# End of an attention and spectral-filter kernel: other order of the output projections' products, other banks for the last memory terms, last rows stored by halves of columns

## Chip, cores and metric

One core of one Trainium2 chip runs the kernel. The metric is device time in microseconds, the median of three executions. One further execution was recorded by the hardware profiler; its page and trace are what is quoted here.

## What is computed

Two independent parts on one input sequence of 2048 rows and 576 columns each, concatenated. Part A is attention with 32 heads of width 18 in four segments of 512 rows, with a running memory M, z, and an output projection with `wo`:

```python
for s in range(N):                      # 4 segments
    qs, ks, vs = q[:, :, s], k[:, :, s], v[:, :, s]
    logits = jnp.einsum("bhqd,bhkd->bhqk", qs, ks) * scale + mask
    p = _softmax(logits, axis=-1)
    a_dot = jnp.einsum("bhqk,bhkd->bhqd", p, vs)
    pq = phi(qs)
    num = jnp.einsum("bhld,bhde->bhle", pq, M)
    den = jnp.einsum("bhld,bhd->bhl", pq, z)[..., None] + 1e-6
    a_mem = num / den
    o = g * a_mem + (1.0 - g) * a_dot
    ...                                 # M, z take in this segment's keys and values
return o @ wo
```

Part B is `irfft2(rfft2(x) * W)`, a filter in the two-dimensional spectrum. The change touches part A alone.

## The kernel before

**Stages.** Forward transform of part B; the projections q, k, v of part A beside the middle of part B; the inverse transform; and then the attention, from `attention` (line 925), which runs to the end of the program. The instructions of each engine stand in the order in which the Python code issues them (a manual schedule); the framework adds the semaphore waits and assigns buffers. Nothing is moved at run time: an engine whose next instruction waits holds up everything behind it on that engine.

**The attention loop.** 133 steps t (lines 947 to 1014), one per head up to step 127. A step interleaves, on TensorE: `s1` (row maxima for the head ten steps ahead), `s2` (line 679: scores with the maximum subtracted, three banks p0, p1, p2 from the tag "s2", which ScalarE turns into exponentials P at lines 688, 693, 697), `pv` (line 708: P times values) and a background list that `run_bg` steps through. The background list holds, for each finished segment, `combine` (line 803: o = memory term plus scaled attention, in five tiles of up to 126 rows, the last of 72), `mem1` (line 786: the next segment's memory terms: the product pn, copied by ScalarE, then pb, the reciprocal spread over the head's rows, multiplied by VectorE) and `oproj` (line 847: the output projection).

**Two words for each value.** The projections keep about 24 bits: o and `wo` are each split in a high word and the rest, so a block is three products, oh x woh, oh x wol and ol x woh, for each of the five tiles t. oh is ScalarE's cast of the combined tile (line 817; line 872 in the last segment), ol the difference that VectorE (or GpSimd) makes behind it (lines 812 and 876). `oproj` has four row blocks `tb` by two column halves `hf` of 288 columns: 15 products into one bank, with a point after the eighth at which other work is put in.

**The last segment.** It has no attention left to hide behind. `last_tile` (line 864) makes o for one tile: pb, two VectorE steps, the cast to oh, and, one tile later, ol through `last_low`. `last_proj` (line 884) issues the three products of accumulator u and tile t. Eight accumulators u (four row blocks by two halves) are open at once: 0 to 2 in the banks of tag "s1", 3 in "pv", 4 to 6 in "s2", 7 in "post". The order is tile 0 for u = 0 to 6, then tile 1, then tile 2 (with the `last_tile` of tiles 3 and 4 put in), then tile 3, then u = 7 for tiles 0 to 3, then tile 4 for all eight; behind each accumulator's last product ScalarE (even u) or VectorE (odd u) copies it to a row block in SBUF, and after each odd one SP stores the row block of 128 x 576.

**Banks.** TensorE's results lie in eight banks: three of tag "s1", three of "s2", one "pv", one "post". `bank` (line 783) gives `oproj`, `combine` and `mem1` a bank of "post" while the step number `s.now` is under 119, and one of "s1" after that. A new use of a bank waits for the engine that reads the old one.

**Queues.** SP issues all loads and stores of this part in program order; a DMA whose source is not ready holds up those behind it on SP.

Of the kernel before, what the change touches and what calls it, by code (L numbers as in the profile page):

```python
# [5 lines left out]
F32=mybir.dt.float32; F32R=mybir.dt.float32r  # L6
# [96 lines left out]
class FFT:  # L103
# [4 lines left out]
    def forward(s,xp,cp,pp,wl,xs,consts):  # L108
# [26 lines left out]
        def f1(u):  # L135
            p=pp.tile([128,2,512],F32,name="f1",tag="f1")
            h,l=eh.pop(u),el.pop(u)
            for r in range(2):
                L=[(h[:,r,0],tab[:,0,r,0]),(h[:,r,1],tab[:,0,r,1]),(h[:,r,0],tab[:,1,r,0]),(h[:,r,1],tab[:,1,r,1]),
                   (l[:,r,0],tab[:,0,r,0]),(l[:,r,1],tab[:,0,r,1]),(h[:99,r,2],tab2[:99,r])]  # L140
                for n,(x,t) in enumerate(L):
                    nc.tensor.matmul(p[:,r,:FP],x,t,start=n==0,stop=n==6)  # L142
# [59 lines left out]
    def bf(s,x,y,inv):  # L202
# [4 lines left out]
        for o,a,b,op in ((t[0],x[0],x[2],OP.add),(t[1],x[0],x[2],OP.subtract),(t[2],x[1],x[3],OP.add),(t[3],x[1],x[3],OP.subtract),  # L207
# [3 lines left out]
            yield  # L211
    def tws(s,L,inv):

        nc=s.nc; v=nc.vector; A=[]; L=[x for x in L if x[1]]
        if not L: return
        for i in range(len(L)+1):
            if i<len(L):
                y,e=L[i]; a=-2*np.pi*e/16*(-1 if inv else 1)
                if i%2==0: T=s.tp.tile([128,2,2,FP],F32,name="tw",tag="t",bufs=4)
                t=T[:,i%2]  # L220
                nc.scalar.activation(t[:,0],y[:,1],AF.Copy,scale=-float(np.sin(a)))
                nc.scalar.activation(t[:,1],y[:,0],AF.Copy,scale=float(np.sin(a)))
                A.append((y,t,float(np.cos(a))))
                if i==0: yield
            if i>0:
                y,t,c=A.pop(0)
                v.scalar_tensor_tensor(y,y,c,t,op0=OP.mult,op1=OP.add)
                yield
# [161 lines left out]
class ATT:  # L390
# [391 lines left out]
        lane.append(chain())  # L782
    def bank(s,name,r=126):

        return (s.ps if s.now<119 else s.ps1).tile([r,512],F32,name=name,tag="post" if s.now<119 else "s1")
    def mem1(s,g,t):
        nc=s.nc; r=126 if t<4 else 72
        pn=s.bank("pn")
        nc.tensor.matmul(pn[:r],s.Mst[g][:r,t,:r],s.pq.pop((g,t))[:r],start=True,stop=True)
        am=s.tp.tile([126,512],F32,name="am",bufs=5)  # L790
        nc.scalar.copy(am[:r],pn[:r])
        if g<3: s.later(1,lambda: s.pq_load(g+1,t))
        yield
        pb=s.bank("pb")
        nc.tensor.matmul(pb[:r],s.sel[:,t,:r],s.rc["rd"],start=True,stop=True)
        nc.vector.tensor_tensor(am[:r],am[:r],pb[:r],op=OP.mult)
        s.am[t]=am; s.amg[t]=g
        yield
# [48 lines left out]
    def oproj(s,g):  # L847
        nc=s.nc
        oh,ol=s.oh,s.ol
        for tb in range(4):  # L850
            ob=s.tp.tile([128,576],F32,name="ob")
            c=slice(128*tb,128*tb+128)
            for hf in range(2):
                ps=s.bank("po",128)[:,:288]
                w=slice(288*hf,288*hf+288)
                L=[(a,b,t) for a,b in ((oh,s.woh),(oh,s.wol),(ol,s.woh)) for t in range(5)]
                for i,(a,b,t) in enumerate(L):
                    r=126 if t<4 else 72
                    nc.tensor.matmul(ps,a[t][:r,c],b[:r,t,w],start=i==0,stop=i==14)  # L859
                    if i==7: yield  # L860
                nc.scalar.copy(ob[:,w],ps)
                if hf==1: s.later(1,lambda tb=tb,ob=ob: nc.sync.dma_start(s.io["ya"][g*512+128*tb:g*512+128*tb+128],ob))
                yield
# [14 lines left out]
    def last_parts(s):  # L878
# [2 lines left out]
        c=c.rearrange("p a b -> p (a b)")  # L881
        s.oh=[a[:,t] for t in range(4)]+[c[:,:512]]; s.ol=[b[:,t] for t in range(4)]+[c[:,512:]]
        s.lows=[]; s.acc={}
    def last_proj(s,u,t):

        nc=s.nc; tb,hf=divmod(u,2); c=slice(128*tb,128*tb+128); w=slice(288*hf,288*hf+288); r=126 if t<4 else 72
        if t==0: s.acc[u]=(s.ps1 if u<3 else s.ps).tile([128,512],F32,name="po",tag="s1" if u<3 else "pv" if u==3 else "s2" if u<7 else "post")[:,:288]
        for i,(a,b) in enumerate(((s.oh,s.woh),(s.oh,s.wol),(s.ol,s.woh))):
            nc.tensor.matmul(s.acc[u],a[t][:r,c],b[:r,t,w],start=t==0 and i==0,stop=t==4 and i==2)  # L889
    def later(s,k,f):  # L890

        s.late.append((s.now+k,f))
# [32 lines left out]
    def attention(s,tp,ps):  # L925
        nc=s.nc; s.tp,s.ps,s.psm,s.mtag=tp,ps,s.ps1,"s1"
# [19 lines left out]
        for t in range(133):  # L946
# [24 lines left out]
            a=s.s1(t+10) if t+10<128 else iter(())  # L971
            b=s.s2(t) if t<128 else iter(())
# [5 lines left out]
            r=(t-5)%4  # L978
# [4 lines left out]
            if t==129:  # L983
                for j in range(4): s.pv(31,j)
                s.pv_out(31)
                u=s.u_dmas(15)
# [6 lines left out]
            if 7<=t<131 and t%4==3:  # L993
                s.pv_out((t-7)//4)
                if t%8==3:
                    u=s.u_dmas((t-11)//8)
# [31 lines left out]
                s.last_proj(u,t)  # L1028
                if t==2 and u in (1,4): s.last_tile(3 if u==1 else 4,"re")
        s.last_low()  # L1030
        for u in range(7): s.last_proj(u,3)
        for t in range(4): s.last_proj(7,t)
        o=[s.tp.tile([128,4,512],F32,name=f"P{i}").rearrange("p a b -> p (a b)") for i in range(2)]
        o=[o[tb//3][:,576*(tb%3):576*(tb%3)+576] for tb in range(4)]
        nc=s.nc
        for u in range(8):
            tb,hf=divmod(u,2); s.last_proj(u,4)
            (nc.vector.tensor_copy if hf else nc.scalar.copy)(o[tb][:,288*hf:288*hf+288],s.acc[u])
            if hf: nc.sync.dma_start(s.io["ya"][1536+128*tb:1664+128*tb],o[tb])

def prio(tc,gen,off):

# [99 lines left out]
```

## Time and profile before

| | us |
|---|---|
| median of 3 executions | 714.35 |
| lowest, highest | 713.14, 716.41 |
| profiled execution, as timed | 714.98 |
| its span, first to last instruction | 713.3 |
| last product on TensorE starts | 709.25 |
| last copy out of a bank starts, takes | 709.65, 0.46 |

In a timeline row stand the start, the duration (a matmul's includes its way through the array, so rows of matmuls overlap), engine, line, operation, result and operands, shapes, how many, and in square brackets how long the engine stood idle before it and which instruction released it. In the chain of waits stand start, length and what ran. A row of the windows gives a stretch, its length, the busy time of TensorE, its weight loads (PEld), VectorE (DVE), ScalarE (ACT) and GpSimd (POOL), the granted TensorE clock, the share of the 16 DMA engines that was busy, and GB/s. The granted clock was 1.00 from 640 to 691 us and 0.99 from 691 to 713.

### The profile page before, as it was taken

The page shows a single profiled execution, that of the slowest core. Times are in us where ns is not written, and L with a number is a line of the kernel's source. Part 1 is how long each engine was busy: PE and PEld are TensorE (multiplying, and loading weights), DVE is VectorE, ACT ScalarE, POOL GpSimd, SP SyncE. Part 2 cuts the span into 40 slices and gives each one's busy share as a digit, 9 for nine tenths or more (in the row PEclk, how much of TensorE's full clock was granted, in tenths as well). Part 3 has the DMA queues.
Part 4 walks back from the last instruction along what each step waited for, and adds up shares of the span by engine and source line. Part 5 has one row for each costly group of instructions (what it writes and reads, how often), then busy time and mean ns, then how long its engine had stood idle before and what let it go on. Part 6 is the DMA issues. An engine that isn't in the chain of part 4 may idle for free.

```text
span 713.3 us, 14181 instructions
## 1 busy us (share of the span) xinstructions
PE 678.1 (95%) x4867; PEld 498.7 (70%) x4867; DVE 553.9 (78%) x1227; ACT 444.5 (62%) x1000; POOL 209.8 (29%) x409
## 2 busy tenths in 40 slices
PE   4999999999999999999999999999999999998997
PEld 3999779879889889999744444444566445664677
DVE  5999989989899887887588878887666876668153
ACT  3657796585584564444387777777656776568631
POOL 2110000100100211565065434545242762237200
PEclk9999999999999999999999999999999999999999
DMA  9877436555463568889637666677547765341331
GB/s 322 276 233 216 142 125 201 189 171 172 158 221 127 164 220 270 214 235 210 172 105 181 169 162 154 175 177 175 133 121 181 170 167 131 103 138 43 99 100 66
DMA packets 83244, 121.04 MB, mean 170 GB/s; under 512 B 11352, under 2 KB 50630, under 8 KB 83036
## 3 DMA queue, kind: packets, MB, share of 16 engines
q1 hardware_dynamic: 76580, 104.11, 51.8%
q0 software_dynamic: 6592, 16.03, 7.9%
q8 instruction: 38, 0.62, 0.4%
q14 instruction: 34, 0.28, 0.1%
HBM read 81.78 MB, written 38.24 MB: 168 GB/s over the span
## 4 chain that ended last, share of the span: by engine, by line
PE 67%; DVE 12%; DMA 7%; ACT 7%; issue 5%; POOL 2%; SPq 0%; DVEq 0%; ACTq 0%; POOLq 0%
PE pv L717 10%; PE pj L464 9%; PE pjv L464 8%; PE po L859 7%; PE s L644 5%; PE s L652 4%; PE i L300 3%; DMA yb<-yout 3%; PE s L687 3%; PE i L311 3%; DVE junk L648 3%; PE s L691 2%; PE po L889 2%; DMA xin<-xb 2%; PE c L163 2%
## 5 line engine op out<-in xcount | busy, mean ns | idle before, releaser
L648 DVE CUSTOM_DVE_ANT_0 junk<-s,mask 128x512 bf16<-128x512 f32 (+1 forms) x256 | 141.8, 554 | 56.4 <-PE s L644 45.4
L654 DVE TENSOR_REDUCE mx<-s 128x4 f32<-128x512 f32 x128 | 87.9, 687 | 17.2 <-PE s L653 15.5
L688 ACT ACTIVATE P<-s 128x512 f32<-128x512 f32 x128 | 77.2, 603 | 23.3 <-PE s L687 20.6
L717 PE MATMUL pv<-P,vs 128*32 128x512 f32 (+3 forms) x1024 | 82.0, 438 | 0.0
L693 ACT ACTIVATE P<-s 128x512 f32<-128x512 f32 x128 | 77.0, 601 | 6.8 <-PE s L692 3.6
L697 ACT ACTIVATE P<-s 128x256 f32<-128x256 f32 x128 | 49.6, 388 | 50.1 <-PE s L696 50.0
L700 POOL TENSOR_SCALAR_AFFINE_SELECT P<-P 128x512 f32<-128x512 f32 x116 | 69.5, 636 | 6.2 <-ACT P L688 6.0
L717 PEld LDWEIGHTS pv<-P,vs 128*32 128x32 f32 x1024 | 26.8, 109 | 44.6 <-issue 41.9
L464 PE MATMUL pj<-x,wqkh 128*128 128x512 f32 x162 | 56.0, 406 | 0.0
L514 POOL MEMSET vt<- 128x32 f32 x16 | 2.4, 162 | 149.6 <-PE pm L524 122.3
L210 DVE TENSOR_TENSOR t<-Z 128x580 f32<-128x580 f32 x64 | 46.2, 757 | 0.1
L210 DVE TENSOR_TENSOR Z<-t 128x580 f32<-128x580 f32 x64 | 45.9, 755 | 0.0
L644 PE MATMUL s<-Ks,Qs 108*128 108x512 bf16 (+1 forms) x128 | 42.2, 329 | 0.0
L142 PE MATMUL f<-ftab,eh 128*128 128x290 f32 (+1 forms) x160 | 31.3, 314 | 10.4 <-DMA ftab<-ftab 10.4
L300 PE MATMUL i<-civ,Y 128*128 128x256 f32 (+1 forms) x288 | 37.8, 284 | 0.8 <-DVE T L332 0.8
L488 ACT CAST sp<-pj 128x512 bf16<-128x512 f32 x36 | 21.1, 586 | 27.0 <-DVE pj L484 27.0
L311 PE MATMUL i<-itab,T 128*128 128x290 f32 (+1 forms) x224 | 36.6, 312 | 1.0 <-DVE yout L319 1.0
L669 POOL CAST mh<-mg 128x16 bf16<-128x16 f32 x32 | 6.9, 216 | 101.1 <-ACT mg L667 69.2
L300 PEld LDWEIGHTS i<-civ,Y 128*128 128x128 f32 (+1 forms) x288 | 35.8, 181 | 1.0 <-DVE T L332 1.0
L464 PE MATMUL pj<-xh,wqkh 128*128 128x512 f32 x90 | 35.6, 395 | 0.0
L464 PEld LDWEIGHTS pj<-x,wqkh 128*128 128x128 f32 x162 | 30.4, 188 | 7.4 <-issue 0.6
L464 PE MATMUL pj<-x,wqkl 128*128 128x512 f32 x90 | 35.5, 395 | 0.0
(214 smaller groups left out, 1856.5 us busy)
## 6 DMA issues: line engine op xcount, KB each, us to landing
qkD<-sp SPq DMA_DIRECT2D x36, 384.0 KB
Ks<-qkD SPq DMA_DIRECT2D x72, 144.0 KB
x<-qkD SPq DMA_DIRECT2D x60, 144.0 KB
Qs<-qkD SPq DMA_DIRECT2D x60, 144.0 KB
xin<-xb SPq DMA_DIRECT2D x16, 384.0 KB
cfw<-cfw POOLq DMA_DIRECT2D x16, 384.0 KB, 4.9
civ<-civ POOLq DMA_DIRECT2D x16, 384.0 KB, 7.4
vs<-vD SPq DMA_DIRECT2D x16, 330.0 KB
```

The costliest lines, as they stand in the source:

```text
L210: v.tensor_tensor(o,a,b,op=op)
L300: nc.tensor.matmul(p[:m,k],Y[i][:,q,c*128:c*128+m],cc[:,hl,o:o+256],start=n==0,stop=n==5)
L311: nc.tensor.matmul(p,x,t,start=n==0,stop=n==6)
L464: s.nc.tensor.matmul(out,a,b,start=i==0,stop=i==len(L)-1)
L644: nc.tensor.matmul(out,Q[:108,h,128*i:128*i+128],K[:108,h,:128*(i+1)],start=True,stop=True)
L648: nc.vector.tensor_tensor_reduce(out=junk[:,:w],in0=src,in1=s.mask[:,512-w:],scale=1.0,scalar=-3.0e38, op0=OP.add,op1=OP.max,accum_out=s.m ...
L654: nc.vector.tensor_reduce(out=s.mx[k][:,hh],in_=pa.rearrange("p (b c) -> p b c",c=128),axis=mybir.AxisListType.X,op=OP.max)
L688: nc.scalar.activation(P[0][:,hh],p0,AF.Exp,scale=SC)
L693: nc.scalar.activation(P[1][:,hh],p1,AF.Exp,scale=SC)
L700: if k<29: nc.gpsimd.affine_select(out=x,in_=x,pattern=pat+[[1,128]],compare_op=OP.is_ge,fill=0.0,base=0,channel_multiplier=-1)
L717: nc.tensor.matmul(s.pvt[32*hh:32*hh+32,128*j:],vt[:,j,19*h:19*h+32],mv[0][:,hh,mv[1]],start=j==0,stop=j==2,skip_group_check=True)
L859: nc.tensor.matmul(ps,a[t][:r,c],b[:r,t,w],start=i==0,stop=i==14)
```

## The change

Four edits. `bank` gives, once the step number is over 130, a bank of tag "s2", which the exponentials no longer use. `oproj` takes the two products of oh's tile 4 behind those of tiles 0 to 3. `last_proj` can issue its oh products (part 0) and its ol product (part 1) apart; tile 3 is done for u = 0 to 6 with the oh products first and then all ol products, and so are accumulators 0 to 2 of tile 4. The last row block is stored by two DMAs of 128 x 288, the first behind the copy of accumulator 6, the second behind that of 7.

```diff
--- before.py
+++ after.py
@@ -782,7 +782,7 @@
         lane.append(chain())
     def bank(s,name,r=126):
 
-        return (s.ps if s.now<119 else s.ps1).tile([r,512],F32,name=name,tag="post" if s.now<119 else "s1")
+        return (s.ps if s.now<119 or s.now>130 else s.ps1).tile([r,512],F32,name=name,tag="post" if s.now<119 else "s1" if s.now<131 else "s2")
     def mem1(s,g,t):
         nc=s.nc; r=126 if t<4 else 72
         pn=s.bank("pn")
@@ -853,7 +853,7 @@
             for hf in range(2):
                 ps=s.bank("po",128)[:,:288]
                 w=slice(288*hf,288*hf+288)
-                L=[(a,b,t) for a,b in ((oh,s.woh),(oh,s.wol),(ol,s.woh)) for t in range(5)]
+                L=[(oh,b,t) for T in (range(4),(4,)) for b in (s.woh,s.wol) for t in T]+[(ol,s.woh,t) for t in range(5)]
                 for i,(a,b,t) in enumerate(L):
                     r=126 if t<4 else 72
                     nc.tensor.matmul(ps,a[t][:r,c],b[:r,t,w],start=i==0,stop=i==14)
@@ -881,11 +881,12 @@
         c=c.rearrange("p a b -> p (a b)")
         s.oh=[a[:,t] for t in range(4)]+[c[:,:512]]; s.ol=[b[:,t] for t in range(4)]+[c[:,512:]]
         s.lows=[]; s.acc={}
-    def last_proj(s,u,t):
+    def last_proj(s,u,t,part=None):
 
         nc=s.nc; tb,hf=divmod(u,2); c=slice(128*tb,128*tb+128); w=slice(288*hf,288*hf+288); r=126 if t<4 else 72
         if t==0: s.acc[u]=(s.ps1 if u<3 else s.ps).tile([128,512],F32,name="po",tag="s1" if u<3 else "pv" if u==3 else "s2" if u<7 else "post")[:,:288]
         for i,(a,b) in enumerate(((s.oh,s.woh),(s.oh,s.wol),(s.ol,s.woh))):
+            if part is not None and part!=(a is s.ol): continue
             nc.tensor.matmul(s.acc[u],a[t][:r,c],b[:r,t,w],start=t==0 and i==0,stop=t==4 and i==2)
     def later(s,k,f):
 
@@ -1028,15 +1029,18 @@
                 s.last_proj(u,t)
                 if t==2 and u in (1,4): s.last_tile(3 if u==1 else 4,"re")
         s.last_low()
-        for u in range(7): s.last_proj(u,3)
+        for part in range(2):
+            for u in range(7): s.last_proj(u,3,part)
         for t in range(4): s.last_proj(7,t)
         o=[s.tp.tile([128,4,512],F32,name=f"P{i}").rearrange("p a b -> p (a b)") for i in range(2)]
         o=[o[tb//3][:,576*(tb%3):576*(tb%3)+576] for tb in range(4)]
         nc=s.nc
+        for u in range(3): s.last_proj(u,4,0)
         for u in range(8):
-            tb,hf=divmod(u,2); s.last_proj(u,4)
+            tb,hf=divmod(u,2); s.last_proj(u,4,None if u>2 else 1)
             (nc.vector.tensor_copy if hf else nc.scalar.copy)(o[tb][:,288*hf:288*hf+288],s.acc[u])
-            if hf: nc.sync.dma_start(s.io["ya"][1536+128*tb:1664+128*tb],o[tb])
+            w=slice(0,576) if u<6 else slice(288*hf,288*hf+288)
+            if hf or u==6: nc.sync.dma_start(s.io["ya"][1536+128*tb:1664+128*tb,w],o[tb][:,w])
 
 def prio(tc,gen,off):
```

The instructions on VectorE, ScalarE and GpSimd stay in their order; SP has one DMA more, at its end; TensorE has the same products in another order. In the rows below `P0` holds oh's and `P1` ol's tiles 0 to 3 of the last segment, `P2` both of tile 4, and a row's brackets name the engine or DMA whose semaphore it waits for.

TensorE, the first half of segment 2's first half-projection in `oproj`, at the step in which oh is being made (`oh_9043` is tile 3, `oh_9053` tile 4). Before:

```order
L859 MATMUL po_9065<-woh_4318,oh_9008 128x288
L859 MATMUL po_9065<-woh_4318,oh_9043 128x288 [waits Activation_49]
L859 MATMUL po_9065<-woh_4318,oh_9053 128x288 [waits Activation_49]
L859 MATMUL po_9065<-wol_4319,oh_8939 128x288
L859 MATMUL po_9065<-wol_4319,oh_8991 128x288
L859 MATMUL po_9065<-wol_4319,oh_9008 128x288
L687 LDWEIGHTS Ks3_3182
L687 MATMUL s2_9074<-x0_2659,Ks3_3182 128x512
L691 LDWEIGHTS Ks3_3182
L691 MATMUL s2_9077<-x0_2659,Ks3_3182 128x384 [waits Activation_49]
```

Now:

```order
L859 MATMUL po_9065<-woh_4318,oh_9008 128x288
L859 MATMUL po_9065<-woh_4318,oh_9043 128x288 [waits Activation_49]
L859 MATMUL po_9065<-wol_4319,oh_8939 128x288
L859 MATMUL po_9065<-wol_4319,oh_8991 128x288
L859 MATMUL po_9065<-wol_4319,oh_9008 128x288
L859 MATMUL po_9065<-wol_4319,oh_9043 128x288
L687 LDWEIGHTS Ks3_3182
L687 MATMUL s2_9074<-x0_2659,Ks3_3182 128x512 [waits Activation_49]
L691 LDWEIGHTS Ks3_3182
L691 MATMUL s2_9077<-x0_2659,Ks3_3182 128x384 [waits Activation_49]
```

Tile 4's product has gone out of the first half, to the head of the second (it stands with its wol product behind the next L687 there); tile 3's wol product has come in. The scores of `s2` behind the half are the same; L687 now shows its own wait for an exponential, which the wait for the cast stood for before.

TensorE, the last pb of `mem1` and the first product of each accumulator of `last_proj`. Before:

```order
L795 MATMUL pb_9440<-rd_8751,sel_4316 72x512 [waits Activation_49]
L889 MATMUL po_9444<-woh_4318,P0_9344 128x288 [waits DVE_49]
...
L889 MATMUL po_9448<-woh_4318,P0_9344 128x288 [waits Activation_49]
...
L889 MATMUL po_9452<-woh_4318,P0_9344 128x288 [waits DVE_49]
...
L889 MATMUL po_9456<-woh_4318,P0_9344 128x288 [waits PE_49]
...
L889 MATMUL po_9460<-woh_4318,P0_9344 128x288
...
L889 MATMUL po_9464<-woh_4318,P0_9344 128x288
...
L889 MATMUL po_9468<-woh_4318,P0_9344 128x288
```

Now:

```order
L795 MATMUL pb_9440<-rd_8751,sel_4316 72x512 [waits Activation_49]
L890 MATMUL po_9444<-woh_4318,P0_9344 128x288
...
L890 MATMUL po_9448<-woh_4318,P0_9344 128x288
...
L890 MATMUL po_9452<-woh_4318,P0_9344 128x288
...
L890 MATMUL po_9456<-woh_4318,P0_9344 128x288 [waits PE_49]
...
L890 MATMUL po_9460<-woh_4318,P0_9344 128x288 [waits DVE_49]
...
L890 MATMUL po_9464<-woh_4318,P0_9344 128x288 [waits Activation_49]
...
L890 MATMUL po_9468<-woh_4318,P0_9344 128x288 [waits DVE_49]
```

The pb waits for ScalarE as before. The three waits that stood at the first three accumulators now stand at accumulators 4 to 6, in the banks of "s2".

TensorE, tile 3 of the last segment: before the start of it, and of now the place at which the oh products end and the ol products begin.

```order
L889 MATMUL po_9468<-woh_4318,P0_9344 128x288
L889 MATMUL po_9468<-wol_4319,P0_9344 128x288
L889 MATMUL po_9468<-woh_4318,P1_9345 128x288
L889 MATMUL po_9444<-woh_4318,P0_9344 128x288 [waits Activation_49]
L889 MATMUL po_9444<-wol_4319,P0_9344 128x288
L889 MATMUL po_9444<-woh_4318,P1_9345 128x288 [waits DVE_49]
L889 MATMUL po_9448<-woh_4318,P0_9344 128x288
L889 MATMUL po_9448<-wol_4319,P0_9344 128x288
L889 MATMUL po_9448<-woh_4318,P1_9345 128x288
```

```order
L890 MATMUL po_9464<-woh_4318,P0_9344 128x288
L890 MATMUL po_9464<-wol_4319,P0_9344 128x288
L890 MATMUL po_9468<-woh_4318,P0_9344 128x288
L890 MATMUL po_9468<-wol_4319,P0_9344 128x288
L890 MATMUL po_9444<-woh_4318,P1_9345 128x288 [waits DVE_49]
L890 MATMUL po_9448<-woh_4318,P1_9345 128x288
L890 MATMUL po_9452<-woh_4318,P1_9345 128x288
```

Before, the third product already needed ol (it waits for VectorE). Now fourteen products with oh stand ahead of the first that needs it.

## The prediction, made before the changed kernel ran

> **What bounds the kernel now.** I read the page first, then the chain of waits in order of time for the last 60 us (the change touches nothing else that waits), then the timelines of the engines named there.
>
> ```profile
> span 713.3 us, 14181 instructions
> PE 678.1 (95%) x4867; PEld 498.7 (70%) x4867; DVE 553.9 (78%) x1227; ACT 444.5 (62%) x1000; POOL 209.8 (29%) x409
> PE 67%; DVE 12%; DMA 7%; ACT 7%; issue 5%; POOL 2%; SPq 0%; DVEq 0%; ACTq 0%; POOLq 0%
> ```
>
> TensorE is busy 95% of the span and is two thirds of the chain. The change removes no product; it can only win what TensorE stands idle, and that is little. The chain shows where:
>
> ```profile
> 655.50 0.63 ACT oh L817
> ...
> 656.64 0.50 ACT oh L817
> ...
> 657.18 0.80 PE po L859 x4
> ...
> 686.01 0.23 PE pb L869
> 686.24 0.67 DVE am L796
> ...
> 690.81 0.31 ACT ob L861
> ...
> 691.16 0.38 PE pb L795
> 691.54 6.69 PE po L889 x48
> ...
> 701.30 0.61 DVE P L876
> ...
> 701.96 7.61 PE po L889 x55
> ...
> 709.65 0.46 DVE P L1038
> ```
>
> The reader is to see four places where the chain leaves TensorE: at 656 (a cast of oh), from 686.24 to 691.16 (a run of VectorE and ScalarE work that ends in a bank's release), at 701 (a subtraction that makes ol) and at the end (copy and store). From 657.18 to 686.24 every piece is TensorE, and the run after it starts behind a TensorE product, so time won at 657 should arrive at 691.
>
> The pace of products comes from two rows 51 products apart:
>
> ```profile
> 702.32 0.29 PE L889 MATMUL po<-wol,P 126*128 126x288 f32 x1
> ...
> 709.12 0.29 PE L889 MATMUL po<-wol,P 72*128 72x288 f32 x1
> ```
>
> 6.80 / 51 = 0.133 us for each product, with 126 rows or with 72.
>
> **Step A: `oproj`, other order of 15 products.** All 24 half-projections change, but over the whole run line 859 waited for a cast of oh only here:
>
> ```profile
> 656.19 0.40 PE L859 MATMUL po<-woh,oh 126*128 126x288 f32 x1 [0.33 <-ACT oh L817]
> 657.18 0.40 PE L859 MATMUL po<-woh,oh 72*128 72x288 f32 x1 [0.60 <-ACT oh L817]
> ...
> 657.82 0.39 PE L687 MATMUL s<-x,Ks 110*128 110x512 bf16 x1
> 658.05 0.33 PE L691 MATMUL s<-x,Ks 110*128 110x384 bf16 x1
> ...
> 657.02 0.60 ACT L693 ACTIVATE P<-s 128x512 f32<-128x512 f32 x1
> ...
>   ACT oh L817: 2.3, 4
> ```
>
> The last row is the whole run's list for line 859: four waits, the two here seen by the products and again by their weight loads. The first (tile 3) stays, since tile 3 is still the fourth product. The second (tile 4, 72 rows) goes: the slot after 656.19 is 656.32, tile 4's product ran at 657.18, so 0.86 us was lost; now four products with wol fill it to 656.85. Behind them stand L687 and, 0.23 us later, L691, which needs the bank that ScalarE's L693 frees at 657.02 + 0.60 = 657.62. It can start at about 657.66 and not at 657.08, against 658.05 now: the wait for the cast is replaced in part by one for the exponential behind it in ScalarE's queue. I take 0.39 us; the ends are 0 (what is won is lost again in the VectorE run before 691) and 0.86. The ol products keep their places, and the other 23 half-projections only swap products of one price.
>
> **Step B: the last memory terms in other banks.** Three banks rotate as before, so the last pb still waits for the copy L861 at 690.81; that stall stays. What changes is that the first three accumulators of `last_proj` find free banks. Before, they took the banks of the last pb, pn and pb, and the third waited for
>
> ```profile
> 691.64 0.68 DVE L796 TENSOR_TENSOR am<-am,pb 72x512 f32<-72x512 f32 x1 [0.29 <-ACT am L791]
> ```
>
> Up to the next pb the chain gives 6.69 us for 48 products; 48 x 0.133 = 6.40. So 0.29 us goes. The waits move to accumulators 4 to 6, at least 12 products (1.6 us) later, at 693.1; the row above ends at 692.32, so they are covered with 0.8 us to spare. Ends: 0 and 0.3.
>
> **Step C: tile 3's products in two parts.** This is the largest term.
>
> ```profile
> 700.36 0.64 PE L889 MATMUL po<-woh,P 126*128 126x288 f32 x2
> 700.83 0.30 PE L889 MATMUL po<-wol,P 126*128 126x288 f32 x1
> 701.96 0.53 PE L889 MATMUL po<-woh,P 126*128 126x288 f32 x2 [0.82 <-DVE P L876]
> ...
> 701.22 1.51 DVE L876 TENSOR_TENSOR P<-ux,P 126x512 fp32r<-126x512 f32 x2
> ...
> 701.39 0.62 ACT L872 CAST P<-ux 72x512 fp32r<-72x512 f32 x1 [0.84 <-DVE ux L871]
> ```
>
> After the product at 700.83 the next slot is 700.96; the ol product ran at 701.96, when the first of the two subtractions was done. 1.00 us lost. Now 13 more products that need only oh fill 700.83 to 702.56, and ol is ready at 701.91: the wait is covered with 0.65 us to spare. What could be late next is tile 4: its oh is ready at 702.01, its ol at 702.73, and 19 products stand ahead of it, so it is asked for at 705.1. I take the whole 1.00; its lower end is 0.8, if the two engines run a little later against TensorE. Without the cover it would cost the 1.00 again.
>
> **Step D: the end.** The last products are also reordered: accumulators 0, 1, 2 now end with the 7th, 8th and 9th of 24 and not the 3rd, 6th and 9th; 3 to 7 end as before. The last block is stored in two halves, the first behind ScalarE's copy, the second behind VectorE's.
>
> ```profile
> 707.19 0.46 DVE L1038 COPY P<-po 128x288 f32<-128x288 f32 x1 [4.46 <-PE po L889]
> ...
> 707.72 2.80 SPq L1039 DMA_DIRECT2D ya<-P  x4
> ...
> 707.50:708.50 1.00, 1.00 (x10) 1.00 (x9) 0.60 (x2) 0.52 (x2) 0.00 (x0) 1.00 0.00 0
> 708.50:709.50 1.00, 1.00 (x8) 0.81 (x7) 0.46 (x1) 0.54 (x2) 0.00 (x0) 1.00 0.90 346
> 709.50:710.00 0.50, 0.05 (x1) 0.00 (x0) 0.35 (x1) 0.14 (x1) 0.00 (x0) 1.00 0.99 382
> 710.00:710.50 0.50, 0.00 (x0) 0.00 (x0) 0.11 (x1) 0.00 (x0) 0.00 (x0) 1.00 0.96 364
> 710.50:711.00 0.50, 0.00 (x0) 0.00 (x0) 0.00 (x0) 0.00 (x0) 0.00 (x0) 1.00 0.88 332
> 711.00:711.50 0.50, 0.00 (x0) 0.00 (x0) 0.00 (x0) 0.00 (x0) 0.00 (x0) 1.00 0.91 355
> 711.50:712.00 0.50, 0.00 (x0) 0.00 (x0) 0.00 (x0) 0.00 (x0) 0.00 (x0) 1.00 0.61 235
> ```
>
> In these rows the column before the last is the share of the 16 DMA engines. From 708.5, some 0.8 us after the first issue, to about 711.8 they are 88 to 99% busy: share times width sums to 3.08 us, 0.77 for each of four stores. The stores already stand end to end. Accumulator 1 now ends two products later, so the first store starts 0.27 us later, and the row of stores behind it is as long as before; a shorter last piece then ends nothing sooner. The 0.27 us of gaps between 708.5 and 711.85 take up a part of the delay: I take a loss of 0.15 us. The lower end is a gain of 0.38, half a store's time, if the engines find room for the last half. The upper end is the whole 0.27 and what the rows of the halves cost, which have 1152 bytes and not 2304:
>
> ```profile
> q1 hardware_dynamic: 76580, 104.11, 51.8%
> ```
>
> 51.8% of 16 engines over 713.3 us, by 76580 packets, is 77 ns for a packet of 1360 bytes on average; a store's row takes 0.77 us / 8 = 96 ns. Two half rows at no more than 77 ns are 58 ns dearer, eight times 0.46 us: a loss of 0.73 in all. SP issues five stores and not four; each waits for its copy, and the 2.80 above is mostly that waiting.
>
> The Trainium skill (DMA: Bandwidth & Descriptors, Anatomy of one DMA) splits a transfer into a fixed 2.0 us and bytes over 436 GB/s; by it a last piece of 147 KB would end 0.34 us sooner, and the sum below would be 2.0. The same skill (Perfetto Trace Analysis, DMA Optimizations) has splitting help where the DMA engines are generally idle; by the shares of 0.88 to 0.99 here they are not, and I follow the trace.
>
> **Sum.** 0.39 + 0.29 + 1.00 - 0.15 = 1.53 us. The profiled execution took 714.98 us, 0.63 above the median of 714.35; its span was 713.3 and 1.7 lies around it, which the change leaves alone. Off the median: 714.35 - 1.53 = 712.8 us.
>
> **Rivals.**
> 1. The halves end the stores sooner: D as a gain of 0.38, 2.06 us in all, 712.3; with A at 0.86 too, 2.5 us, 711.8. For it: the gaps between stores. Against: the shares, and for A the row of L693. 15%.
> 2. A and B are swallowed by the run of VectorE and ScalarE rows before 691, which is fed by reloads through SP and not only by TensorE; C stays: 0.85 us, 713.5. For it: at 686.24 the chain does leave TensorE. 22%.
> 3. The change does not do what it says at C: the stall moves to tile 4 or into the extra products' banks, and only the 0.29 of B and half of A are left against D: 0.3 us, 714.0. Against: 0.65 and 2.4 us of cover. 8%.
> 4. The slow one: each half-projection's second half now starts with a 72-row weight load behind a bf16 product. A load takes 188 ns:
>
> ```profile
> L859 PEld LDWEIGHTS po<-woh,oh x120: 186/188/201, 504.3 to 687.5; 126*128 126x128 f32 x96, 72*128 72x128 f32 x24
> ```
>
> If it lies open in all 24, that is 4.5 us; less 1.5 it is 714.35 + 3.0 = 717.3. It decides from 0.06 us a time on. Against: the pace is equal for 72 and 126 rows, and every first half already begins with such a switch. 4%.
>
> The forecast has 48%; 3% is left for what I do not see.
>
> **How the numbers follow.** The three runs shown lie between 713.14 and 716.41, so a median of a few runs can stand 1.5 us off by itself. The likeliest case with that spread is 711.3 to 714.4; with rivals 1 to 3 and the bounds above (A, B, C and D at their best a gain of 2.5; at their worst 0 + 0 + 0.8 - 0.73, no gain) the range is 710.7 to 715.4. A measurement of this kernel can tell a change from none at about 0.5%, 3.57 us: none of the first three cases reaches 710.78, only a run's own spread on top of rival 1 would, 5%. Rival 4 alone comes near 717.92: 3%. The rest, 92%, is no change that can be told.
>
> **What would show it.** Right: no wait for L817 of 0.6 us at tile 4, but L691 right behind an exponential (A); 48 products in 6.4 us behind the last pb of tile 4 (B); no wait on L876, and from there to the last product no hole but the one for tile 3's oh (C); DMA shares over 0.9 from the first store to the last, ending 2.2 to 2.5 us behind the last product (D; 709.54 to 711.85 now). Wrong: a half-projection's second half over 0.2 us longer; the last pb later against the products ahead of it; a gain above 2.6 or any loss above 1 us.

## The result, and the profile after

| | before | after |
|---|---|---|
| median, us (20 executions each) | 715.22 | 712.52 |
| lowest, highest | 712.0, 721.82 | 711.32, 715.68 |
| ratio to before | | 0.9962, 95% interval 0.9945 to 0.9979 |
| span of the profiled execution | 713.3 | 710.3 |

712.52 us stands beside the forecast of 712.8. The medians differ by 2.7 us, more than the 1.53 us of the sum, and the two spans by 3.0. Before any step is judged, it has to be asked where in the two executions these 3.0 us lie. The last transposition of the row maxima (L673) stands 60 us ahead of the end, ahead of all but the segment 0 and 1 part of the change. Timeline of TensorE, before:

```profile
652.31 0.23 PE L673 MATMUL mt<-idb,mh 128*128 128x128 bf16 x1 [0.70 <-POOL mh L670]
```

and after:

```profile
651.04 0.23 PE L673 MATMUL mt<-idb,mh 128*128 128x128 bf16 x1 [0.70 <-POOL mh L670]
```

1.27 of the 3.0 us are already there. The change moves nothing ahead of the first half-projection of `oproj`, whose first product starts at 504.31 us before and at 503.18 after: 1.13 us of the difference is older than the change. The largest piece of it is one wait: at 348.99 us TensorE had stood idle for VectorE for 1.02 us (L311) in the profiled execution of the kernel before, and not in that of the changed one. So each run below is read by stretches between fixed instructions, not by its span. From L673 to the last instruction it was 60.96 us and is now 59.24: **1.72 us**.

The chain of waits after, in order of time:

```profile
654.24 0.63 ACT oh L817
...
655.37 0.50 ACT oh L817
655.87 0.51 ACT P L693
656.37 0.04 issue
656.41 0.32 PE s L691
...
689.14 0.31 ACT ob L861
689.45 0.04 issue
689.49 0.38 PE pb L795
689.87 6.38 PE po L890 x48
...
697.88 8.59 PE po L890 x63
...
706.56 0.46 DVE P L1041
```

The reader is to see three things against the chain before. Behind the cast at 655.37 the chain now goes on with the exponential L693 and reaches TensorE at L691, as step A had it: one wait in ScalarE's queue has handed over to the next. The pb at 689.49 still waits for the copy L861, and the 48 products behind it take 6.38 us and not 6.69 (B). And from 697.88 TensorE runs 63 products without a break where VectorE's subtraction stood in the chain before (C). The end, in the windows (the column before the last is the share of the DMA engines):

```profile
705.30:705.60 0.30, 0.30 (x4) 0.30 (x3) 0.06 (x1) 0.30 (x1) 0.00 (x0) 1.00 0.00 0
705.60:706.60 1.00, 0.86 (x7) 0.62 (x5) 0.49 (x2) 0.49 (x2) 0.00 (x0) 1.00 0.82 318
706.60:707.60 1.00, 0.00 (x0) 0.00 (x0) 0.42 (x1) 0.00 (x0) 0.00 (x0) 1.00 1.04 394
707.60:708.60 1.00, 0.00 (x0) 0.00 (x0) 0.00 (x0) 0.00 (x0) 0.00 (x0) 1.00 1.00 366
708.60:709.00 0.40, 0.00 (x0) 0.00 (x0) 0.00 (x0) 0.00 (x0) 0.00 (x0) 0.97 0.77 254
```

The DMA engines have no gap left: from 705.6 on their shares times the widths of the rows sum to 3.2 us, and TensorE is busy in only the first 0.86 us of this.

### The profile page after: what moved, and what is told of

Read it like the earlier page. It is cut to its first block, busy times and chain, and to the rows that moved or that the text cites. A ratio compares the mean times of both kernels' runs of the same rounds, so it can differ in the third digit from the quotient of the medians.

```text
span 710.3 us, 14182 instructions
## 1 busy us (share of the span) xinstructions
PE 677.0 (95%) x4867; PEld 498.7 (70%) x4867; DVE 553.9 (78%) x1227; ACT 444.3 (63%) x1000; POOL 209.7 (30%) x409
## 4 chain that ended last, share of the span: by engine, by line
PE 70%; DVE 10%; DMA 7%; ACT 6%; issue 4%; POOL 2%; SPq 1%; DVEq 0%; ACTq 0%; POOLq 0%
PE pv L717 9%; PE pj L464 9%; PE pjv L464 7%; PE po L859 6%; PE s L644 5%; PE i L300 4%; PE i L311 4%; PE s L652 3%; PE f L142 3%; PE s L687 3%; PE po L890 2%; DVE junk L648 2%; PE s L691 2%; PE c L163 2%; DMA x<-qkD 2%
## 5 line engine op out<-in xcount | busy, mean ns | idle before, releaser
L693 ACT ACTIVATE P<-s 128x512 f32<-128x512 f32 x128 | 77.0, 602 | 6.8 <-PE s L692 3.5
L311 PE MATMUL i<-itab,T 128*128 128x290 f32 (+1 forms) x224 | 36.4, 311 | 0.0
```

The costliest lines, as they stand in the source:

```text
L311: nc.tensor.matmul(p,x,t,start=n==0,stop=n==6)
L693: nc.scalar.activation(P[1][:,hh],p1,AF.Exp,scale=SC)
```

## The experiments

Every row below is read from one profiled execution, cut at the starts of the same products (us):

| kernel | first `oproj` product at | from there to L673 | L673 to the end | of it: L673 to first `last_tile` pb | to last `mem1` pb | to tile 3's pb | to the last product | to the end |
|---|---|---|---|---|---|---|---|---|
| before | 504.31 | 148.00 | 60.96 | 32.17 | 6.68 | 6.90 | 11.19 | 4.01 |
| after | 503.18 | 147.86 | 59.24 | 31.77 | 6.68 | 6.59 | 10.08 | 4.12 |
| e1_oproj | 503.29 | 147.86 | 60.54 | 31.77 | 6.68 | 6.90 | 11.19 | 4.00 |
| e2_banks | 507.48 | 149.26 | 60.65 | 32.17 | 6.68 | 6.59 | 11.20 | 4.01 |
| e3_tile3 | 501.94 | 147.99 | 59.84 | 32.18 | 6.68 | 6.90 | 10.08 | 4.00 |
| e4_halves | 503.28 | 148.01 | 60.83 | 32.15 | 6.68 | 6.90 | 11.19 | 3.91 |
| e5_order | 503.25 | 147.99 | 61.03 | 32.17 | 6.68 | 6.90 | 11.19 | 4.10 |
| e6_noorder | 503.48 | 147.88 | 59.02 | 31.75 | 6.68 | 6.59 | 10.07 | 3.91 |
| e7_late7 | 504.29 | 147.86 | 58.71 | 31.76 | 6.68 | 6.59 | 10.09 | 3.59 |
| e8_split_banks | 501.45 | 147.87 | 57.80 | 31.76 | 5.73 | 6.63 | 10.09 | 3.58 |
| e9_early_tiles | 502.44 | 148.00 | 57.57 | 31.76 | 5.73 | 4.24 | 12.25 | 3.59 |
| e10_after_again | 506.52 | 148.02 | 59.27 | 31.76 | 6.67 | 6.60 | 10.10 | 4.14 |

(In e9 tile 3's pb stands 18 products earlier, so its two columns are to be added: 16.49 against 16.72 in e8.) The five columns on the right agree within 0.03 us wherever two kernels have the same instructions there; the first column differs by 6 us between kernels whose instructions up to there are the same. The 149.26 of e2 in the second column is no work of its change, which begins behind L673: the granted clock was 0.50 from 504 to 510 us in that execution alone, and in no other below 0.99 in any 10 us from 420 to 660.

**e1: step A alone.**

```diff
-                L=[(a,b,t) for a,b in ((oh,s.woh),(oh,s.wol),(ol,s.woh)) for t in range(5)]
+                L=[(oh,b,t) for T in (range(4),(4,)) for b in (s.woh,s.wol) for t in T]+[(ol,s.woh,t) for t in range(5)]
```

> Only step A: the new order of the 15 products in oproj. Measured from the last transposition of the maxima (L673, the end stretch: 60.96 us before, 59.24 with the whole change) to the last instruction. Theory 1 (my step A: 0.39 us at one place, the other 23 half-projections neutral, and the 1.1 us by which the changed kernel's execution was already ahead when it reached its first changed instruction is only the spread of executions): end stretch 60.57, and from the first oproj product to L673 no more than 0.2 us less than before. Theory 2 (the new order wins in the half-projections of segments 0 and 1 as well): that middle stretch is 1 us shorter or more. Theory 3 (the run of VectorE and ScalarE work before 691 swallows it): end stretch 60.96.

Measured: 60.54, and 0.40 of the 0.42 lies between L673 and the first pb of `last_tile`. Theory 1 holds, and what was won at one place did arrive (theory 3 falls). The stretch ahead of L673 is 0.14 us shorter here and in four more kernels with the new order, but not in e9 and e10, which have it too: there single longer waits take it up (at 565.77 us in e9 the product pn waits 0.15 us longer for VectorE than in e8, at 596.82 us in e10 pd waits 0.17 us for a reload of pq). No whole microsecond is won there, and theory 2 falls. The 0.14 us do not arise at one place, no single step is over 0.04 us; where they come from stays open.

**e2: step B alone.**

```diff
-        return (s.ps if s.now<119 else s.ps1).tile([r,512],F32,name=name,tag="post" if s.now<119 else "s1")
+        return (s.ps if s.now<119 or s.now>130 else s.ps1).tile([r,512],F32,name=name,tag="post" if s.now<119 else "s1" if s.now<131 else "s2")
```

> Only step B: the last memory terms in the banks of s2. Theory 1: 48 products behind the last pb of mem1 take 6.4 us and not 6.7, the 0.6 us wait of that pb for the copy stays; end stretch 60.67 (0.29 less). Rival: the banks do more, the wait of the last pb goes too, 0.6 us more: 60.0.

Its chain of waits:

```profile
695.25 0.31 ACT ob L861
695.55 0.04 issue
695.60 0.38 PE pb L795
695.97 6.38 PE po L889 x48
...
705.42 0.61 DVE P L876
706.04 0.04 issue
706.08 7.61 PE po L889 x55
```

The 48 products take 6.38 us, the pb still hangs on the copy, and the subtraction L876 is still in the chain, since step C is not in this kernel. 0.31 us: theory 1.

**e3: step C alone.**

```diff
-        for u in range(7): s.last_proj(u,3)
+        for part in range(2):
+            for u in range(7): s.last_proj(u,3,part)
```

> Only step C: tile 3 with all oh products ahead of the ol products. Theory 1: the wait for L876 (0.82 us in the list, 1.0 us of lost slots) goes; end stretch 59.96. Rival: the wait moves to tile 4 or to the accumulators' copies: less than 0.5 us gained, 60.5 or more.

The same place in its chain is one piece,

```profile
697.27 0.22 PE pb L869
697.49 8.59 PE po L890 x63
```

as in the changed kernel. 1.11 us, all of it between tile 3's pb and the last product; the wait moved nowhere.

**e4 and e5: the two halves of step D.** e4 stores the last block by halves and leaves the products alone; e5 has the reorder of tile 4 and stores the block whole.

```diff
-            if hf: nc.sync.dma_start(s.io["ya"][1536+128*tb:1664+128*tb],o[tb])
+            w=slice(0,576) if u<6 else slice(288*hf,288*hf+288)
+            if hf or u==6: nc.sync.dma_start(s.io["ya"][1536+128*tb:1664+128*tb,w],o[tb][:,w])
```

> Only the store of the last row block by halves, products in the old order. Theory 1 (the DMA engines are full from the first store on): the last half goes out as the queue lets it, 0.1 to 0.2 us sooner; end stretch 60.8. Rival (a transfer has a fixed part and one by size, the engines have room): half a store's time, 0.38 us: 60.58.

```diff
+        for u in range(3): s.last_proj(u,4,0)
         for u in range(8):
-            tb,hf=divmod(u,2); s.last_proj(u,4)
+            tb,hf=divmod(u,2); s.last_proj(u,4,None if u>2 else 1)
```

> Only the reorder of tile 4 (accumulators 0 to 2: oh products first), the last row block stored whole. From the last product's start to the last instruction it is 4.01 us before, 4.12 with the whole change, 3.91 with the halves alone. Theory 1 (full DMA engines: the first store starts two products, 0.27 us, later and all behind it follow): 4.2 to 4.28. Rival (gaps in the queue take it up): 4.01.

From the last product to the end: 3.91 with the halves (0.10 won, theory 1), 4.10 with the reorder (0.09 lost). That is midway between theory 1's 4.20 and the rival's 4.01, so neither was right: of the 0.27 us by which the first store is later, the gaps between stores take up two thirds. Both together are 4.12, not 4.00: once the reorder has closed the gaps, the halves win nothing.

**e6: the whole change without the reorder.** The diff is that of e5, taken back.

> The whole change without the reorder of tile 4. Theory 1 (the reorder is the part that costs): the last stretch is 3.91 as with the halves alone, the end stretch from L673 59.03 against 59.24. Rival (tile 4's ol is late without the reorder, now that TensorE arrives 1.1 us sooner): a wait for L876 before tile 4, 59.24 or more.

59.02, the last stretch 3.91; no wait for tile 4's ol appears. The reorder is the one part of the change that costs: 0.09 us by itself (e5), and 0.21 in the whole change (4.12 against 3.91), since behind it the 0.10 us of the halves is lost as well.

**e7: stores sooner.** Accumulator 7's twelve early products go behind accumulator 5's last.

```diff
-        for t in range(4): s.last_proj(7,t)
...
-        for u in range(3): s.last_proj(u,4,0)
         for u in range(8):
-            tb,hf=divmod(u,2); s.last_proj(u,4,None if u>2 else 1)
+            tb,hf=divmod(u,2)
+            if u==6:
+                for t in range(4): s.last_proj(7,t)
+            s.last_proj(u,4)
```

> As e6, and accumulator 7's products of tiles 0 to 3 (12 products, 1.6 us) are put behind accumulator 5's last instead of ahead of tile 4, so that three of the four row blocks are stored 1.6 us sooner. Theory 1 (the stores stand in a full queue at the end): the queue is empty when the last half comes, the last stretch is 3.6, the end stretch 58.7. Rival (the end is the fixed part of a transfer alone): 3.9, 59.0. If tile 4's oh or ol is late, a wait for L872 or L876 shows and it is longer.

Its windows at the end, as above:

```profile
704.00:705.00 1.00, 1.00 (x10) 1.00 (x8) 0.51 (x2) 0.60 (x2) 0.00 (x0) 1.00 0.02 9
705.00:706.00 1.00, 1.00 (x10) 1.00 (x9) 0.46 (x1) 0.20 (x1) 0.00 (x0) 1.00 0.96 371
706.00:707.00 1.00, 1.00 (x10) 1.00 (x9) 0.00 (x0) 0.00 (x0) 0.00 (x0) 1.00 0.98 376
707.00:708.00 1.00, 0.55 (x5) 0.32 (x3) 0.34 (x1) 0.40 (x1) 0.00 (x0) 1.00 0.34 129
708.00:709.00 1.00, 0.00 (x0) 0.00 (x0) 0.12 (x1) 0.00 (x0) 0.00 (x0) 1.00 0.42 149
709.00:710.80 1.80, 0.00 (x0) 0.00 (x0) 0.00 (x0) 0.00 (x0) 0.00 (x0) 0.64 0.24 81
```

The transfers of three row blocks now run beside TensorE's last 2 us. From 707 to 708 the share falls to 0.34, and only the two halves of the last block follow. The last stretch is 3.59: 0.32 less than in e6, from which only the place of the twelve products differs, and 0.53 less than with the whole change, which has the reorder as well. So the queue of stores was a bound at the end. What the halves by themselves are worth behind an empty queue is not shown: no run stores the last block whole with the other stores moved ahead.

**e8: the wait that the change left.** The pb at 689.49 waits because it gets the bank of `oproj`'s last sum. Here `oproj` keeps the banks of "s2" and `mem1` those of "s1" from step 131 on.

```diff
     def bank(s,name,r=126):
...
+        if s.now>130: return (s.ps if name=="po" else s.ps1).tile([r,512],F32,name=name,tag="s2" if name=="po" else "s1")
...
-        if t==0: s.acc[u]=(s.ps1 if u<3 else s.ps).tile([128,512],F32,name="po",tag="s1" if u<3 else "pv" if u==3 else "s2" if u<7 else "post")[:,:288]
+        if t==0: s.acc[u]=(s.ps1 if 3<u<7 else s.ps).tile([128,512],F32,name="po",tag="s2" if u<3 else "pv" if u==3 else "s1" if u<7 else "post")[:,:288]
```

> As e7, and from step 131 on oproj's sums lie in the banks of s2 and mem1's in those of s1, with the accumulators' banks swapped to match, so that the last pb takes a bank that was read long before and not that of oproj's last sum. Theory 1 (the 0.6 us wait for L861 is the bank alone): from the first pb of last_tile to the last pb of mem1 5.9 us and not 6.68, end stretch 57.9. Rival (the same VectorE and ScalarE work is waited for one step later, at the first accumulators): 5.9 there, but 0.4 to 0.8 us more behind it; 58.3 to 58.7.

Its chain, at the same place:

```profile
686.11 0.86 PE pn L790 x2
686.97 0.22 PE pb L796
687.19 6.41 PE po L891 x48
```

No copy, no cast: TensorE goes from pn to pb to the accumulators. The stretch is 5.73 and not 6.68, 0.95 us less where 0.78 was expected, and the accumulators pay back 0.04. The VectorE and ScalarE run in the chain before was there only through the banks that `oproj` and `mem1` shared.

**e9: the last hole.** The wait for tile 3's oh, by making the last two tiles earlier.

```diff
-                if t==2 and u in (1,4): s.last_tile(3 if u==1 else 4,"re")
+                if t==1 and u in (2,5): s.last_tile(3 if u==2 else 4,"re")
```

> As e8, and the last two tiles of last_tile are made earlier: behind accumulators 2 and 5 of tile 1 instead of 1 and 4 of tile 2. Theory 1 (the 0.2 us for tile 3's oh is the last hole of TensorE, and re and ux have long landed): the hole goes; end stretch 57.6 against 57.80, and the time 0.9950 to 0.9965 of before by the stretch alone (60.96 - 57.6 = 3.4 us of 714, 0.5%), since the spread of executions before the first changed instruction is the same for both. Rival (re or ux land later than the earlier pb asks for them): a wait for a DMA at L870 or L871, 57.8 or more.

The end stretch is 57.57. The wait of 0.2 us for the cast L872, which e8's list of waits still has, is gone, and the chain has one piece to the end of the products:

```profile
693.75 0.22 PE pb L870
693.97 10.76 PE po L891 x81
```

This kernel beats both: 709.44 us (six executions, 709.02 to 710.57) against 713.97 before (seventeen, 712.2 to 716.47), ratio 0.9939, interval 0.9924 to 0.9953; on the same chip the twelve of the changed kernel lie between 711.47 and 719.52. The ratio is below the 0.9950 to 0.9965 that was expected. The stretch explains 3.39 of these 4.5 us, a ratio of 0.9953 at the very end of the interval; the other 1.1 us are not explained.

**e10: the changed kernel once more**, on the same chip and beside the same executions of the kernel before as e9.

> The changed kernel once more, beside the version above on the same chip. Theory 1 (the change is worth what the end stretch shows, 1.72 us or 0.24%, and 0.14 us in the middle from the new order in oproj): ratio 0.9975, interval round it. Rival (something else is won, as the first ratio of 0.9962 would say): 0.9960.

Ratio 0.9996, interval 0.9977 to 1.0016; end stretch 59.27, 1.69 us less than before. Neither the 0.9975 of theory 1 nor the rival's 0.9960 lies in that interval. The two ratios of the change, 0.9962 and 0.9996, stand on either side of 0.9976, which 1.7 us of 714 would give; the first interval (0.9945 to 0.9979) holds it and not 1, the second begins just above it and holds 1. By the times alone the size of the change is not settled. The chain shows a part of what the spread is made of. This execution, ahead of the first changed product:

```profile
497.44 0.86 PE pn L789 x2
498.38 6.33 DMA pq<-pqD
504.84 1.02 PE pd L771 x2
...
506.68 1.16 PE po L859 x8
```

and the first execution of the same kernel:

```profile
494.65 0.88 PE pn L789 x2
...
501.50 1.02 PE pd L771 x2
...
503.34 1.16 PE po L859 x8
```

The first product of `oproj` came 3.3 us later than in the other execution. A reload of pq landed so late that the chain goes through it, but the product pn ahead of it was already 2.79 us later (497.44 against 494.65). Only 0.55 us arise at pd, where TensorE waited 1.26 us for the reload and 0.71 us for an exponential in the other execution. The rest are single waits further ahead, the largest at 398.03 us: 1.58 us for a reload of Ks, against 0.34. All of them stand ahead of the change.

## Why the prediction was right

The time, 712.52 for 712.8, and the forecast of a change too small to tell (0.38% by the medians) were right; and by the stretches the steps were too. That the time came within 0.3 us is in part luck. The forecast stands on the 714.35 us of the first three executions; the median of twenty is 715.22, and off that the same sum would have given 713.7, 1.2 us too much. And one sign of being wrong that the prediction names, a gain above 2.6 us, was there: 2.70 by the medians and 3.0 by the spans. Of the 3.0 us, 1.13 lie ahead of the first `oproj` product, 0.14 between there and L673, and 1.72 in the end stretch, where the steps are.

- **A**, 0.39: measured 0.40, in `after` and in e1. That the wait would hand over to the exponential behind the cast is in the chain word for word; the 0.86 of rival 1 did not come.
- **B**, 0.29: 0.31. The pb's wait for L861 stayed, as said.
- **C**, 1.00: 1.11. The term was a tenth too small: I counted the lost slots (0.133 us each) but not that the products right behind the wait came slower. Before, the two products from 701.96 on took 0.36 us to the next row at 702.32 and not 0.27.
- **D**, a loss of 0.15: a loss of 0.11. The reasoning held in its direction: the reorder costs, and behind it the halves win nothing (4.10 without them in e5, 4.12 with them). By themselves they do win 0.10 (e4), which the term had at nothing. The gaps took up two thirds of the first store's 0.27 us; I had taken less than half.
- **Sum**, 1.53: 1.72 in the end stretch.

The rivals: 2 (A and B swallowed ahead of 691) falls with e1 and e2, whose gains arrive whole; the run of VectorE and ScalarE work it rested on was tied to TensorE through a bank, as e8 shows. 3 falls with e3. 4 (an open weight load in all 24 second halves, 4.5 us) falls with the stretch to L673, in which 16 of them lie: it is 147.86 to 148.02 us in the kernels with the new order and 148.00 before. Rival 1's gain of 0.38 us by the halves did not come: e4 won 0.10. Nor did the estimate of 0.34 us for them, by the Trainium skill (DMA: Bandwidth & Descriptors, Anatomy of one DMA). That section gives its fit for one transfer on the GpSimd path, and these are several stores issued by SP behind one another. With the stores moved ahead the stretch fell by 0.32 more (e6 to e7), but how much of that belongs to the halves is not shown.

What I had not reckoned with is that the first measured difference, 2.7 us, would be larger than the sum by 1.2 us. The 1.72 us of the stretch lie within the interval of the first ratio (1.5 to 3.9 us), and the excess did not come again in e10; so the spread of the first 504 us is its likeliest source, and not a fifth term. The stretches are read from one execution of each kernel, the medians from twenty, and so this is argued and not shown.

## What to carry to other kernels

Where executions spread by some microseconds, read a change that is worth less by the stretch between two fixed instructions of the profile: here it repeats to 0.03 us while whole times spread by several. Before a late transfer is cut into smaller ones, look whether the queue ahead of it is empty; moving the earlier stores ahead won three times what the cut did by itself (0.32 and 0.10 us). And a wait for a bank names the engine that read it last, but the cure may be to give the waiting product another bank and not to make that engine faster.

## What was unexpected

The start of the first `oproj` product, with the same instructions ahead of it, lay between 501.45 and 507.48 us in twelve executions, at a granted clock of 0.994 to 1.000. In e2 and e10, the latest two, the chain goes through a reload of pq, for 6.8 and 6.33 us; TensorE itself stood idle for it 2.94 us at 504.34 in e2 and 1.26 us at 504.84 in e10. Behind it the granted clock was 0.50 in e2 until 510 us, and the two products pd took 1.89 us; in e10 it stayed at 1.00 and they took 1.02. Whether the longer idle time lowered the clock, and why that reload lands late in some executions, was not tried.
